# A new written order for a fused RWKV-style scan and wave-mixing kernel on one core

## The chip, the cores and the metric

The kernel runs on one core of a Trainium2 chip. The metric is the device time of one execution in microseconds (us). A core has a matrix engine (PE, with a separate row PEld for its weight loads), two elementwise engines that can read the matrix engine's accumulators in PSUM (DVE and ACT), a third one that can only work on SBUF here (POOL, GpSimd), and a queue that issues transfers (SP). Each engine runs its own instructions strictly in the order in which the program lists them and waits on semaphores for the others.

## The reference

For each of 4 x 8 batch-heads a 40 x 40 state is carried over 768 steps; the outputs, laid side by side as a 4 x 768 x 320 tensor `x`, go through a mixing layer:

```
for t in range(S):
    y[t] = r[t] @ state
    Sa   = state @ a[t]
    state = state * w[t] - outer(Sa, b[t]) + outer(v[t], k[t])
theta = x @ w_theta
y = w_tok_r @ (x * cos(theta)) + w_tok_i @ (x * sin(theta))   # over tokens
u = x + y
out = u + relu(u @ w_ch)
```

## The kernel before, in words

The 768 steps are cut into six chunks of 128 for each of the four batches: 24 chunks, numbered 0 to 23. A chunk holds all eight heads. Inside a chunk the recurrence becomes matmuls on a 128 x 128 scale. The decay is summed on PE from log w and exponentiated on ACT (`CSE`, `CSI`, `WI`, `INVW`, once for two chunks); POOL, and for chunks 0 and 1 DVE, multiplies k and b by one decay (`KH`, tile kb) and a by the other (`AH`, tile ah). PE transposes these (`TRK`, `TRA`, `TRV`, `TRR`), DVE or ACT copies the transposes out of PSUM (`EKBT` to kbT, `EAT` to aT, `EVT` and `ERT` to rvT). Four score matrices per chunk (`PSI`, `PHI`, `LV`, `LU`) are triangular: DVE evicts one with a multiplication by a mask (`EPSI` and so on with V), or ACT evicts it as it is (with A) and POOL then zeroes the other half (`MPSI`, `MPHI`, `MLV`, `MLU`). Solved values (`X0`, `NU`), the carried state (`GT`, `EGT`, `GD`, `EGD`) and the output x (`Y`, `EX`) follow. The old state is added to the new one either by a matmul with the identity (`GI`, function `gt_old`) or by an addition on DVE (`EGA`, function `add_gt`).

The mixing layer follows chunk by chunk: x is transposed (`XT`, `EXT`, or `EXT` with S by a transposing transfer on SP), multiplied by w_theta (`TH`), copied (`ETH`), put through the sine table twice on ACT (`SIN`), and multiplied by x on POOL (`ZR`, tile z). `YR:i.j` adds the share of chunk j to the token mix of chunk i, two matmuls of 320 columns; `EU` adds x, `UT` and `EUT` transpose u, `CH` and `CHR` multiply by w_ch, `EO` makes the output and `ST` stores it. The token-mix sums of chunks 18 to 21 lie in pairs, 18 with 19 and 20 with 21, in one PSUM tile each (the tiles sc0 and sc1, kept in `pairs`); the others have a bank of their own.

What sets the order is one string, `ORDER`. Each entry names a step, its chunk, the engine (A, V, G for POOL, S for a transposing transfer) and a PSUM bank (after @), and the program is recorded in that order with `keep_in_program_order`; nothing is rescheduled. Input loads (`LD..`) stand in the same string, so their order against each other is fixed too. In the names of the trace, sm tiles are single banks and sc tiles two banks; a wait on an sc tile is a wait on the whole tile.

ACT holds one function table at a time: one with ln and exp, one with sin. `ln_exp` loads the first where the last one loaded was another, with a written instruction; before the change the sine table was loaded by one that the compiler puts ahead of a sine.

Of the kernel before, what the change touches and what calls it, by code (L numbers as in the profile page):

```python
# [15 lines left out]
LN_EXP = "natural_log_exp_and_others"  # L16


ORDER = """
LDW:2 LDW:0 LDK:0 LDA:1 LDC:0.0G LDC:0.2G LDA:0 LN:0A LDB:0 CSE:0@0 CSI:0@1 LN:2A CST:0 LDB:1 LDK:1  # L20
INVW:0A WI:0A LDK:2 AH:0V CSI:2@1 CSE:2@0 AH:1V KH:0V CST:2 LDB:2 TRA:0@0 TRK:0@3 LDV:0 EAT:0A
INVW:2A LDR:0 EKBT:0V LDA:2 WI:2A KH:1V PHI:0@1 EPHI:0A PSI:0@0 LDV:1 KH:2G TRA:1@2 EPSI:0V TRK:1@1
EKBT:1V LDB:3 CV:0A MPHI:0G EAT:1A X0:0@0 TRK:2@3 EKBT:2V LDK:3 ENX:0A LDA:3A CR:0A PHI:1@1 PSI:1@0
EPHI:1V LDV:2 AH:2G TRV:0@2 EPSI:1A TRR:0@1 NU:0 LDW:4 EVT:0V ENU:0A TRA:2@3 MPSI:1G GT:0@0 CV:1A
EAT:2V EGT:0V ERT:0A NUT:0@2 LDR:2 PSI:2@0 ENUT:0A PHI:2@1 EPSI:2A TRV:1@3 EPHI:2V KH:3G X0:1@0
LDA:4A ENX:1A LDB:4 LV:0@0 NU:1 EVT:1A LU:0@1 CV:2G ENU:1A ELV:0V TRK:3@2 MPSI:2G ELU:0A NUT:1@3
LDK:4 ERT:1V GT:1@0 GI:1 ENUT:1V LN:4A LV:1@0 LU:1@1 MLU:0G EGT:1V TRV:2@1 LDV:3 X0:2@3 CR:2G ELV:1A
Y:0@0 ELU:1V ENX:2A CSI:4@0 AH:3G LDB:5 EX:0V CSE:4@1 LDA:5A INVW:4A EKBT:3V CST:4 MLV:1G TRA:3@0
LDK:5 WI:4A TRR:2@2 EAT:3V NU:2 EVT:2A ERT:2V KH:4G PSI:3@0 EPSI:3V PHI:3@1 ENU:2A ERT:3A GD:0@0
GT:2@1 LDR:4 NUT:2@3 EGD:0A GI:2 ENUT:2V EPHI:3A LDW:6 TRK:4@2 AH:4G EGT:2V LU:2@0 EKBT:4V CV:3A  # L30
LV:2@1 MPHI:3G X0:3@0 ELU:2A TRA:4@3 Y:1@1 ELV:2V MLU:2G LDA:6A ENX:3A NU:3 EAT:4V TRV:3@2 LDV:4
ENU:3A LDK:6 EX:1V GD:1@3 PHI:4@0 EVT:3V KH:5G PSI:4@1 EGD:1A GT:3@0 EPSI:4A EPHI:4V NUT:3@1 Y:2@2
CR:4G ENUT:3V LN:6A LV:3@0 LDB:6 EX:2V LU:3@1 ELU:3V TRK:5@3 MPSI:4G ELV:3A TRR:4@1 ERT:4A AH:5G
GI:3 GD:2@2 EGT:3V CSE:6@0 LDV:5 CSI:6@1 EGD:2A EKBT:5V CV:4G INVW:6A TRA:5@0 LDK:7 MLV:3G X0:4@2
ENX:4A ERT:5V CST:6 EAT:5V TRV:4@3 XT:1@1 LDB:7 WI:6A XT:0@0 EVT:4V NU:4 KH:6G LDR:6 PHI:5@1 EXT:1A
EXT:0V PSI:5@0 LDA:7A ENU:4A EPHI:5V TH:0@3 AH:6G EPSI:5A NUT:4@0 TRK:6@1 ENUT:4V LDW:8 EKBT:6V
LV:4@1 MPSI:5G LU:4@0 Y:3@2 LDV:6 SIN:0A CV:5G ELU:4V GT:4@0 GI:4 TRV:5@1 KH:7G EGT:4V LDA:8A ELV:4A
EVT:5V MLV:4G TH:1@3 X0:5@0 EX:3V XT:2@1 SIN:1A LDB:8 LV:5@0 TRA:6@2 ENX:5V EXT:2V ELV:5A GD:3@3
EAT:6V TH:2@1 NU:5 CR:6G SIN:2A EGD:3V MLV:5G PSI:6@1 PHI:6@0 ENU:5V EPSI:6V LDV:7 Y:4@2 NUT:5@3
LDK:8 TRR:6@0 ENUT:5V CV:6G EPHI:6V LN:8A TRK:7@1 X0:6@3 LDA:9A ENX:6A AH:7G LU:5@1 ZR:1G LDB:9  # L40
LDK:9 CSE:8@0 ERT:7A ELU:5V NU:6 CST:8 ERT:6A ENU:6A TRA:7@0 ZR:2G EKBT:7V WI:8A AH:8G LDW:10
CSI:8@1 EAT:7V GD:4@3 INVW:8A TRV:6@1 EX:4V PSI:7@0 PHI:7@1 NUT:6@0 EVT:6V EPSI:7V GT:6@2 KH:8G
# [93 lines left out]
def kernel(  # L136
# [14 lines left out]
    nc = tc.nc  # L151
# [176 lines left out]
    table = [LN_EXP]  # L328
# [575 lines left out]
```

## Time and profile before

| | |
|---|---|
| median of three runs | 203.98 us (203.97 to 203.99) |
| profiled execution: its own time, its span | 204.92 us, 203.2 us |
| PE busy | 187.2 us of the span |
| DVE busy | 169.7 us |
| ACT busy | 150.6 us |
| POOL busy | 148.0 us |
| transfers | 35.95 MB, mean 177 GB/s |

The profiled execution is 0.94 us longer than the median, and 1.72 us of it lie outside the span. Busy shares are means over stages with different limits: the head is filled by loads, the first hundred microseconds by elementwise work of the scan, the rest by matmuls of the mixing layer. A PE row's duration includes the way of the last column through the array, so consecutive matmuls overlap in the rows and the distance between two starts says more than a duration.

### The profile page before, as it was taken

The numbers are of one execution on the slowest core, as the hardware profiler recorded it, in microseconds if no ns is written. First come the engines' busy times: TensorE is split into PE (matmuls) and PEld (weight loads), VectorE is DVE, ScalarE is ACT, GpSimd is POOL, SyncE is SP. The second block draws the span as 40 slices with busy tenths as digits, with TensorE's granted clock in tenths as the row PEclk, the third lists the DMA queues.
The fourth block names the chain that finished last, engine by engine and source line by source line (L and its number), as shares of the span: only waits on it lengthen the run. The fifth ranks groups of instructions, "written<-read, shape, count | busy, mean of one in ns | idle before, by whom it ended". The sixth has DMA issues, their size and how long they took to land.

```text
span 203.2 us, 7841 instructions
## 1 busy us (share of the span) xinstructions
PE 187.2 (92%) x3282; PEld 147.9 (73%) x3282; DVE 169.7 (84%) x324; ACT 150.6 (74%) x273; POOL 148.0 (73%) x155
## 2 busy tenths in 40 slices
PE   0669999999999999999999999999999999999892
PEld 0357778877877888787887877877777887777570
DVE  7067889999999998999889899889788888863653
ACT  2556988999899888997999676996798877364110
POOL 8126899999999976998995996974899483762000
PEclk9999999999999999999999999999999999999999
DMA  6999999899899899999878997698793995332523
GB/s 159 169 187 199 207 172 215 137 236 166 163 275 256 158 286 205 243 230 220 224 197 185 236 209 133 135 211 204 145 172 59 218 169 93 77 70 54 194 77 129
DMA packets 141956, 35.95 MB, mean 177 GB/s; under 512 B 136353, under 2 KB 140385, under 8 KB 141921
## 3 DMA queue, kind: packets, MB, share of 16 engines
q1 hardware_dynamic: 120064, 31.57, 73.9%
q10 hardware_dynamic: 20800, 3.28, 9.6%
q0 software_dynamic: 1056, 0.61, 2.2%
q8 instruction: 25, 0.41, 1.0%
q14 instruction: 11, 0.08, 0.2%
HBM read 29.54 MB, written 3.93 MB: 165 GB/s over the span
## 4 chain that ended last, share of the span: by engine, by line
PE 70%; DVE 9%; DMA 7%; ACT 7%; SPq 2%; issue 2%; POOL 1%; ACTq 0%; DVEq 0%; POOLq 0%
PE sm L312 37%; PE sm L316 17%; PE sc L312 16%; DMA raw_v<-in_v_dram 3%; DMA raw_a<-in_a_dram 3%; SPq L363 1%; DVE phi L309 1%; DMA uT<-u_two 1%; DVE lamu L309 1%; DVE rvT L301 1%; ACT lamv L299 1%; ACT cs L737 1%; DVE kbT L301 1%; ACT rvT L299 1%; POOL kb L309 1%
## 5 line engine op out<-in xcount | busy, mean ns | idle before, releaser
L309 POOL TENSOR_TENSOR kb<-raw_kb,invW_two 128x640 bf16<-128x640 f32 x22 | 34.0, 1544 | 13.7 <-DMA raw_kb<-in_b_dram 9.9
L309 POOL TENSOR_TENSOR z<-cs,x_two 128x640 bf16<-128x640 f32 x22 | 30.8, 1404 | 6.9 <-ACT cs L737 5.7
L312 PE MATMUL sm<-z,wtok_r 128*128 128x320 bf16 x120 | 34.6, 300 | 0.0
L312 PE MATMUL sm<-z,wtok_i 128*128 128x320 bf16 x120 | 34.5, 299 | 0.0
L309 DVE TENSOR_TENSOR phi<-sc,mask_p 128x1024 bf16<-128x1024 f32 x17 | 20.7, 1220 | 2.7 <-PE sc L312 2.5
L309 POOL TENSOR_TENSOR ah<-raw_a,Wi_two 128x320 bf16<-128x320 f32 x22 | 19.0, 866 | 3.1 <-issue 2.2
L309 DVE TENSOR_TENSOR psi<-sc,mask_p 128x1024 bf16<-128x1024 f32 x15 | 18.3, 1218 | 0.6 <-PE sc L312 0.5
L312 PE MATMUL sc<-aT,kbT 64*128 64x128 bf16 x384 | 17.0, 225 | 0.9 <-DVE kbT L301 0.8
L309 DVE TENSOR_TENSOR lamu<-sc,mask_p 128x1024 bf16<-128x1024 f32 x14 | 17.1, 1220 | 0.3
L312 PEld LDWEIGHTS <-wtok_r 128*128 128x128 bf16 x144 | 14.0, 97 | 4.6 <-issue 0.5
L312 PEld LDWEIGHTS <-wtok_i 128*128 128x128 bf16 x144 | 14.1, 98 | 4.5 <-issue 1.3
L312 PEld LDWEIGHTS <-rvT 64*128 64x128 bf16 (+1 forms) x272 | 13.8, 94 | 3.5 <-issue 1.4
L312 PEld LDWEIGHTS <-kbT 64*128 64x128 bf16 x384 | 11.7, 98 | 5.8 <-issue 3.4
L316 PE MATMUL sm<-ident,kb 128*128 128x128 bf16 x184 | 15.3, 231 | 0.6 <-DVE kb L309 0.5
L301 DVE COPY kbT<-sm 128x1024 bf16<-128x1024 bf16 x20 | 13.7, 685 | 2.2 <-PE sm L316 2.1
L594 POOL TENSOR_SCALAR_AFFINE_SELECT lamv<-lamv 128x1024 bf16<-128x1024 bf16 x13 | 14.2, 1094 | 1.2 <-ACT lamv L299 1.2
L312 PE MATMUL sm<-kb,lamv 128*128 128x40 bf16 x192 | 15.0, 180 | 0.0
L312 PE MATMUL sm<-kb,lamu 128*128 128x40 bf16 x192 | 14.9, 179 | 0.0
L299 ACT CAST lamv<-sc 128x1024 bf16<-128x1024 f32 x13 | 13.2, 1012 | 1.1 <-PE sc L312 0.8
L312 PE MATMUL sm<-wch,uT 128*128 128x320 bf16 x72 | 13.5, 300 | 0.3 <-DVE uT L301 0.2
L309 DVE TENSOR_TENSOR lamv<-sc,mask_p 128x1024 bf16<-128x1024 f32 x11 | 13.4, 1220 | 0.4 <-PE sc L312 0.4
L312 PE MATMUL sm<-wth,xT 128*128 128x320 bf16 x72 | 13.7, 299 | 0.0
(137 smaller groups left out, 609.7 us busy)
## 6 DMA issues: line engine op xcount, KB each, us to landing
raw_w_two<-in_w_dram SPq DMA_DIRECT2D x12, 320.0 KB, 4.8
raw_kb<-in_k_dram SPq DMA_DIRECT2D x24, 160.0 KB, 4.8
raw_kb<-in_b_dram SPq DMA_DIRECT2D x24, 160.0 KB, 4.6
raw_v<-in_v_dram SPq DMA_DIRECT2D x24, 160.0 KB, 4.9
raw_r_two<-in_r_dram SPq DMA_DIRECT2D x12, 320.0 KB, 5.2
out_dram<-oo SPq DMA_DIRECT2D x24, 160.0 KB, 2.2
raw_a<-in_a_dram ACTq DMA_DIRECT2D x20, 160.0 KB, 5.2
wtok_raw<-in_moe_w_tok_r_dram SPq DMA_DIRECT2D x6, 384.0 KB, 4.6
```

The lines of the kernel that those rows point to most:

```text
L299: keep(nc.scalar.copy(out=out, in_=in_))
L301: keep(eng[e].tensor_copy(out=out, in_=in_))
L309: keep(eng[e].tensor_tensor(out=out, in0=in0, in1=in1, op=ALU.mult))
L312: keep(nc.tensor.matmul(out, lhsT=lhsT, rhs=rhs, start=start, stop=stop, skip_group_check=True))
L316: keep(nc.tensor.transpose(out=out, in_=in_, identity=ident))
L363: transfer(queue(e).dma_start(out=tiles[i].raw_kb[:, j], in_=source(ap, i)))
L594: keep(nc.gpsimd.affine_select(out=flat, in_=flat, compare_op=ALU.is_ge, fill=0.0, base=-1, pattern=[[0, 2 * G], [1, 128]], channel_multip ...
L737: keep(nc.scalar.activation(out=cs[i % 5][:, c], in_=tiles[i].theta, func=AF.Sin, bias=(math.pi / 2, 0.0)[c]))
```

## The change

The string is written anew: 1434 entries where there were 1438. The input loads keep their order against each other; the stores and the transposing transfers stand elsewhere between them. Steps change engine: of the 23 `EKBT` evictions by an engine 13 are now on ACT (3 before), of the 24 `EAT` 14 (6), of the 16 `EGD` 7 (13), of the 24 `ENU` 13 (19); ACT casts no more than 3 `CR` (6) and 2 `CW` (3), the rest being POOL's. The masked evictions on DVE are 61 (57 before), those on ACT with a mask step on POOL 35 (39). Five states are added by a matmul (9 before) and 11 on DVE (7). `KH`, `AH` and `ZR` are on the engines on which they were. Two lines of code differ: `sines` loads the sine table by a written instruction where the other one is loaded, and a pair's tile is taken by the first of its two sums instead of the even one.

```diff
 ORDER = """
-LDW:2 LDW:0 LDK:0 LDA:1 LDC:0.0G LDC:0.2G LDA:0 LN:0A LDB:0 CSE:0@0 CSI:0@1 LN:2A CST:0 LDB:1 LDK:1
+LDW:2 LN:2A LDW:0 CSI:2@1 LDK:0 INVW:2A CSE:2@0 LDA:1 LDC:0.0G LDC:0.2G CST:2 LN:0A WI:2A CSE:0@1
...
     def sines(i):
-        table[0] = None
+        if table[0] != SINE:
+            keep(nc.scalar.preload_act_table_set(SINE))
+            table[0] = SINE
...
             else:
-                if j % 2 == 0:
+                if j // 2 not in pairs:
                     pairs[j // 2] = banks(b).rearrange("p a b c -> p a (b c)")
```

Three places show what moves. The first is the start of ACT's queue: the logarithms (lw_two) of the pairs 0/1 (number 93) and 2/3 (number 94), their exponentials, and the first evictions. Before:

```order
L375 ACTIVATE lw_two_0_93<-raw_w_two_210 128x16x40
L375 ACTIVATE lw_two_1_94<-raw_w_two_208 128x16x40
L410 ACTIVATE invW_two_245<-sc1_227 128x640
L452 ACTIVATE Wi_two_247<-sc0_222 128x656
L299 COPY aT_290<-sm0_274 128x256
```

And now:

```order
L375 ACTIVATE lw_two_1_94<-raw_w_two_208 128x16x40
L410 ACTIVATE invW_two_220<-sc1_213 128x640
L375 ACTIVATE lw_two_0_93<-raw_w_two_211 128x16x40
L452 ACTIVATE Wi_two_241<-sc0_222 128x656
L452 ACTIVATE Wi_two_264<-sc1_243 128x656
L410 ACTIVATE invW_two_274<-sc0_259 128x640
L299 COPY aT_291<-sm0_286 128x256
L299 COPY kbT_318<-sm0_304 128x512
```

The pair 2/3 now goes first, its exponential stands ahead of the logarithm of the pair 0/1, and a kbT is copied on ACT.

The second place is the start of DVE's queue behind the memsets: the products of chunks 0 and 1 and the first transposes. Before:

```order
L309 TENSOR_TENSOR ah_0_95<-raw_a_218,Wi_two_247 128x8x40
L309 TENSOR_TENSOR ah_1_96<-raw_a_214,Wi_two_247 128x8x40
L309 TENSOR_TENSOR kb_0_97<-raw_kb_212,invW_two_245 128x16x40
L301 COPY kbT_296<-sm3_279 128x1024
L309 TENSOR_TENSOR kb_1_98<-raw_kb_242,invW_two_245 128x16x40
```

And now:

```order
L309 TENSOR_TENSOR ah_1_96<-raw_a_227,Wi_two_264 128x8x40
L309 TENSOR_TENSOR ah_0_95<-raw_a_257,Wi_two_264 128x8x40
L301 COPY aT_281<-sm0_276 128x512
L309 TENSOR_TENSOR kb_0_97<-raw_kb_218,invW_two_274 128x16x40
L309 TENSOR_TENSOR kb_1_98<-raw_kb_268,invW_two_274 128x16x40
L301 COPY kbT_320<-sm3_294 128x1024
```

Chunk 1's ah goes first and its kb now stands ahead of the copy of chunk 0's kbT.

The third place is near the end of PE's queue: the last token-mix matmuls of chunks 18 and 19, which share one sc0 tile, the first transposes of chunk 18's u (u_two_0), and the products with w_ch between them. Before:

```order
L312 MATMUL sm3_5101<-wch_201,uT_5059 128x320
...
L312 MATMUL sc0_5027<-z_1_199,wtok_i_206 128x320
...
L312 MATMUL sc1_5018<-z_1_199,wtok_r_205 128x320
...
L316 MATMUL sm1_5126<-ident_58,u_two_0_117 128x128
```

And now:

```order
L312 MATMUL sc0_4954<-z_1_199,wtok_i_206 128x320
...
L312 MATMUL sm3_5106<-wch_201,uT_5101 128x320
L312 LDWEIGHTS uT_5101
L312 MATMUL sm1_5122<-wch_201,uT_5101 128x320
...
L312 MATMUL sc1_5005<-z_1_199,wtok_r_205 128x320
...
L312 MATMUL sm2_5001<-z_1_199,wtok_r_205 128x320
...
L316 MATMUL sm1_5137<-ident_58,u_two_0_117 128x128
...
L312 MATMUL sc0_4954<-z_1_199,wtok_r_205 128x320
```

In the old order `YR:18.5`, `EU:18`, `YR:19.5` follow each other with one `YR` of two matmuls (`YR:19.4`, on the same tile) between the first two; in the new one four products with w_ch, six token-mix matmuls of other tiles and two transposes stand between `EU:18` and `YR:19.5`.

More of the change, by code (lines that the diff above doesn't have):

```diff
@@ L16 @@
 LN_EXP = "natural_log_exp_and_others"
+SINE = "trig_and_small"
 ORDER = """
-LDW:2 LDW:0 LDK:0 LDA:1 LDC:0.0G LDC:0.2G LDA:0 LN:0A LDB:0 CSE:0@0 CSI:0@1 LN:2A CST:0 LDB:1 LDK:1
[L21 to L30, printed above, removed]
@@ new lines @@
+EU:0V ENX:10A TRK:11@1 LN:12A NU:10 ELV:10V TH:6@3 CSE:12@1 CW:2.1G MLU:9G EX:8V ENU:10A EKBT:11V
+CSI:12@0 CST:12 LDW:14 LDK:13 ETH:6A GT:10@2 WT:2.1@3 INVW:12A LDB:13 WI:12A WT:2.0@1 EWT:2.1V
+EGA:10V LDA:13A Y:9@0 EWT:2.0A NUT:10@3 XT:8@1 PHI:11@1 KH:12G EGT:10V EXT:8A LDT:3.0 ENUT:10A
+PSI:11@0 YR:2.0@1 EX:9V CV:11A EPSI:11V YR:2.1 XT:9@2 YR:2.2 TRV:11@0 EPHI:11A TRK:12@3 EXT:9V
+EVT:11V X0:11@2 LN:14A LU:10@1 AH:12G LDC:0.4G LV:11@0 LDV:12 MPHI:11G EKBT:12V ELU:10V TRA:12@0
+LDC:0.6G LDR:12 AH:13G ELV:11V YR:2.3 YR:2.4 ENX:11A KH:13G LDA:14A YR:1.0@3 EAT:12A CW:3.0G TH:8@0
@@ new lines @@
+ETH:8V NU:11 YR:2.5 YR:1.1 EU:2V SIN:6A PSI:12@0 PHI:12@1 ENU:11A EPSI:12V YR:1.2 SIN:7A LDB:14
+GD:9@1 LDT:3.1 EPHI:12V TRA:13@2 NUT:11@0 LDK:14 YR:1.3 EAT:13V YR:1.4 CV:12G EGD:9A SIN:8A YR:1.5
+ENUT:11A TRK:13@1 CR:12G LDC:0.5G EKBT:13A CSI:14@0 LU:11@1 LDV:13 X0:12@0 LDC:0.7G EU:1V INVW:14A
+WT:3.0@1 ELU:11V ENX:12V Y:10@3 LDV:14 TRR:12@2 LDR:14 PSI:13@1 LDK:15 NU:12 EWT:3.0V CW:3.1G
+ERT:12A CSE:14@0 EX:10V LDA:15A CST:14 EPSI:13V ENU:12A TRV:12@3 GD:10@1 KH:14G GT:12@0 ERT:13A
+EVT:12V CV:13G LDB:15 WT:3.1@2 WI:14A EGD:10A EWT:3.1A PHI:13@1 LV:12@0 EGT:12V NUT:12@3 ELV:12V
@@ new lines @@
+X0:20@1 ERT:21A YR:9.4 ERT:20V YR:9.5 LN:22A ENX:20V TH:15@3 EU:9V GD:19@2 ST:7 NU:20 EGD:19V
+LV:20@0 ENU:20V CSE:22@1 UT:9@0 YR:11.0@2 SIN:15A CST:22 GT:20@3 YR:11.1 ELV:20V LDB:22 YR:11.2
+WI:22A YR:11.3 EGA:20V CV:21A YR:11.4 MLU:19G AH:22G YR:11.5 PSI:21@0 CSI:22@1 ST:0 CH:8@1 EGT:20V
+EU:11V EUT:9A ENUT:20S EPSI:21V CHR:9@2 CH:9 INVW:22A TRA:22@0 TRV:21@3 EXT:17S PHI:21@1 MLV:19G
+LU:20@0 EO:8V ST:4 EVT:21V EAT:22A ELU:20V TH:17@0 EPHI:21A KH:22G YR:13.0@3 ETH:17A YR:13.1
+TRK:22@1 SIN:16A ZR:15G YR:13.2 EUT:10S MPHI:21G EKBT:22V Y:19@0 LV:21@1 EO:9V UT:11@1 EX:19V
```

193 lines of the change are left out of this document (92 added, 101 removed).

## The prediction

> **What bounds the kernel now.** I read the page first, then the busy time by stage, then what PE waits for, then rows in time at both ends.
>
> ```profile
> span 203.2 us, 7841 instructions
> PE 187.2 (92%) x3282; PEld 147.9 (73%) x3282; DVE 169.7 (84%) x324; ACT 150.6 (74%) x273; POOL 148.0 (73%) x155
> PE   0669999999999999999999999999999999999892
> DVE  7067889999999998999889899889788888863653
> ```
>
> PE is full from the fourth slice to the last three, DVE nearly full up to the middle. A table of stages separates them; the columns are PE, PEld, DVE, ACT and POOL busy time with instruction counts, the clock, and the transfers.
>
> ```profile
> 0.00:20.00 20.00, 11.12 (x130) 8.11 (x131) 11.55 (x54) 9.76 (x16) 9.05 (x20) 1.00 1.01 179
> 20.00:60.00 40.00, 38.40 (x823) 31.18 (x822) 38.09 (x65) 37.27 (x66) 37.84 (x39) 1.00 1.02 196
> 60.00:100.00 40.00, 39.45 (x784) 32.45 (x781) 37.92 (x58) 35.15 (x69) 35.34 (x37) 1.00 1.10 234
> 100.00:180.00 80.00, 79.89 (x1402) 63.53 (x1400) 71.38 (x130) 63.49 (x113) 62.51 (x60) 1.00 0.79 158
> 180.00:203.20 23.20, 18.37 (x154) 12.68 (x152) 10.78 (x23) 4.89 (x14) 3.24 (x3) 1.00 0.35 108
> ```
>
> From 20 to 100 us DVE is busy 38.09 + 37.92 = 76.0 of 80 us and ACT 37.27 + 35.15 = 72.4: the scan's evictions pace PE. From 100 to 180 us PE is idle for 0.11 us in all and DVE for 8.6: PE sets the pace. PE loses 8.9 us in the first 20 us and 4.8 in the last 23. The waits of PE name two causes of size:
>
> ```profile
> PE sc L312 <- ACT lw_two L375: 6.1, 1, 6.1
> PE sc L312 <- DVE u_two L765: 0.9, 2, 0.6
> ```
>
> The first is the head, until the first load has come and its logarithm is made; the second lies in the last stretch. So four terms: the head, the paced first hundred, the matmul stage, the end.
>
> **The head.** Loads keep their order, and ACT's queue now has the exponential of pair 2/3 (`INVW:2`) ahead of the logarithm of pair 0/1 (`LN:0`). Behind `LN:0` wait `CSE:0` on PE, `WI:0` on ACT and the first products on DVE. Rows: a load's time to landing, then instructions with start and duration; the third is a row of the chain of waits.
>
> ```profile
> raw_w_two<-in_w_dram SPq DMA_DIRECT2D x1, 320.0 KB, 3.2
> 5.35 1.36 ACT L375 ACTIVATE lw_two<-raw_w_two 128x640 bf16<-128x640 f32 x2 [3.27 <-DMA raw_w_two<-in_w_dram]
> 3.91 6.05 DMA raw_a<-in_a_dram
> 10.06 0.89 DVE L309 TENSOR_TENSOR ah<-raw_a,Wi_two 128x320 bf16<-128x320 f32 x2 [4.60 <-DMA raw_a<-in_a_dram]
> 12.82 0.69 DVE L301 COPY kbT<-sm 128x1024 bf16<-128x1024 bf16 x1 [1.13 <-PE sm L316]
> ```
>
> The first load (pair 2/3) is issued at 0.8 us and has landed at 4.0; before, its logarithm stood behind the one of pair 0/1, whose load came at 5.3. Now it runs from 4.0 to 4.7, its sums on PE take 0.8 us, `INVW:2` is done near 6.4, `LN:0` runs to 7.1, then sums and `WI:0`, together as long as from 6.7 to 8.7 before, to some 9.2 us. The load of chunk 0's a lands at 3.91 + 6.05 = 9.96 in both orders, so the 1.0 us that `LN:0` comes later is hidden behind that load, with 0.7 us to spare. Chunk 1's ah goes ahead of it for nothing. On DVE the copy of aT and the kb of chunk 1 now stand ahead of the copy of chunk 0's kbT: 0.4 + 0.8 us, in the 1.13 us in which DVE waited for PE before. I take 0. The ends: -1.0, if chunk 1, whose kb and kbT come earlier now, fills PE's gaps between 13 and 20 us; +0.8, if both insertions on DVE (1.2 us) delay the first scores and only 0.4 of it finds cover.
>
> **The first hundred.** I counted the entries ahead of the last output of batch 2 (`EX:11`) in both strings and priced the difference with the grouped rows (busy, mean ns, idle before):
>
> ```profile
> L301 DVE COPY kbT<-sm 128x1024 bf16<-128x1024 bf16 x20 | 13.7, 685 | 2.2 <-PE sm L316 2.1
> L299 ACT COPY kbT<-sm 128x512 f32<-128x512 f32 x3 | 1.8, 588 | 0.7 <-PE sm L316 0.7
> L301 DVE COPY aT<-sm 128x512 bf16<-128x512 bf16 x18 | 7.5, 419 | 1.1 <-PE sm L316 0.9
> L299 ACT COPY aT<-sm 128x256 f32<-128x256 f32 x6 | 2.2, 373 | 3.6 <-PE sm L316 3.6
> L301 DVE CAST gd<-sm 128x320 bf16<-128x320 f32 x3 | 1.5, 484 | 0.3 <-PE sm L312 0.3
> L299 ACT CAST gd<-sm 128x320 bf16<-128x320 f32 x13 | 5.6, 431 | 2.5 <-PE sm L312 2.5
> L563 DVE TENSOR_SCALAR nu<-sm 128x320 bf16<-128x320 f32 x5 | 2.4, 490 | 1.0 <-PE sm L312 0.9
> L644 DVE TENSOR_TENSOR sm<-sm,gt 128x320 f32<-128x320 f32 x7 | 3.4, 491 | 0.3 <-PE sm L312 0.3
> L309 DVE TENSOR_TENSOR phi<-sc,mask_p 128x1024 bf16<-128x1024 f32 x17 | 20.7, 1220 | 2.7 <-PE sc L312 2.5
> L299 ACT CAST lamv<-sc 128x1024 bf16<-128x1024 f32 x13 | 13.2, 1012 | 1.1 <-PE sc L312 0.8
> L299 ACT CAST wtok_row<-wtok_raw 128x768 bf16<-128x768 f32 x3 | 2.5, 833 | 0.0
> L301 DVE COPY rvT<-sm 128x512 bf16<-128x512 bf16 x23 | 12.3, 546 | 0.5 <-ACT rvT L299 0.4
> L312 PE MATMUL sm<-gt,ident 128*128 128x320 bf16 x9 | 2.7, 300 | 0.0
> ```
>
> DVE: kbT -7 x 0.685 = -4.8, aT -4 x 0.419 = -1.7, gd +4 x 0.484 = +1.9, state additions +3 x 0.491 = +1.5, masked evictions +1 x 1.22, nu +2 x 0.490 = +1.0; six small copies change by one, net four fewer at 0.35 to 0.55, -1.8. Together -2.7 us. ACT: kbT +7 x 0.588 = +4.1, aT +4 x 0.373 = +1.5, gd -4 x 0.431 = -1.7, row casts -2 x 0.833 = -1.7, evictions -1.0, small ones +1.4: +2.6 us. POOL has less to do up to there too.
>
> With the busy times above, DVE falls from 76.0 to 73.3 and ACT rises from 72.4 to 75.0. The later one of the two went from 76.0 to 75.0. That is -1.0, and I take -0.9, since two engines near their limit meet more often than one. The ends: -2.7 if ACT's idle time (7.6 us in these 80) swallows its new work; +2.6 if that idle time is all waits for PE in ACT's fixed order and stays, so that its new work is paid in full. PE's own work ahead of that point is the same but for three `GI`.
>
> Rows against rule: a copy of kbT takes 0.685 us on DVE and 0.588 on ACT here. The Trainium skill, "ScalarE: Activation LUTs", section "Rules for kernel authors", gives cheap elementwise work to VectorE, which it calls up to about three times faster per element in bf16. By that rule the seven copies would cost ACT up to 7 x 3 x 0.685 = 14.4 us instead of 4.1, an estimate, and the change would be a loss of some 9 us; the rows contradict it for these copies.
>
> **The matmul stage.** Four `GI` go, one of them (chunk 13) where PE sets the pace. Its row says 0.300 us, but starts of 320 columns lie 0.135 apart (rows below): -0.1. The order within is new; with PE idle for 0.11 us in 80 I take neither gain nor loss; the bounds are 0 (a gain is the second rival) and +1.1, twice the 0.55 us that PE loses in the 40 us from 60 to 100.
>
> **The table.** Loads before:
>
> ```profile
> L737 ACT ACT_TABLE_LOAD x7 | 9.0, 1283 | 0.1
> L332 ACT ACT_TABLE_LOAD x6 | 7.7, 1283 | 0.1
> ```
>
> The new program has seven and six again, each directly ahead of a sine or an exponential on the same queue: 0.
>
> **The end.** Rows of PE, and one of the chain of waits (second):
>
> ```profile
> 188.12 0.97 PE L312 MATMUL sm<-wch,uT 128*128 128x320 bf16 x4
> 186.18 2.42 DMA uT<-u_two
> 188.93 0.30 PE L312 MATMUL sc<-z,wtok_r 128*128 128x320 bf16 x1
> 189.88 0.30 PE L312 MATMUL sc<-z,wtok_i 128*128 128x320 bf16 x1
> 190.76 0.30 PE L312 MATMUL sc<-z,wtok_r 128*128 128x320 bf16 x1 [0.58 <-DVE u_two L765]
> 190.90 0.30 PE L312 MATMUL sc<-z,wtok_i 128*128 128x320 bf16 x1
> 192.40 0.43 PE L312 MATMUL sm<-wch,uT 128*128 128x320 bf16 x2
> 193.14 0.30 PE L312 MATMUL sc<-z,wtok_r 128*128 128x320 bf16 x1 [0.31 <-DVE u_two L765]
> ```
>
> From 190.76 to 190.90 is one matmul: 0.135. The row at 190.76 is `YR:19.5`, which writes the tile that `EU:18` reads; it starts 0.88 after the one at 189.88, so 0.75 is lost. `YR:21.1` at 193.14 waits for `EU:20` alike: 0.74 from 192.40 less two matmuls, 0.47 lost. The four products at 188.12 need 0.54 and the next starts after 0.81: 0.27 lost, on chunk 17's u, whose transfer lands at 186.18 + 2.42 = 188.60. Sum 1.49.
>
> In the new order twelve matmuls of 0.135 stand between the end of `YR:18.5` and `YR:19.5`, ten of them 320 columns wide: 1.4 us, against 0.3 of matmul tail and 0.49 of `EU` (with another `EU` of 0.49 ahead of it). Between `YR:20.5` and `YR:21.2` there are six: 0.8 us, against the same 0.8. `EU:17` is made much earlier, but its transfer now stands behind that of chunk 23's x on SP, so the 0.27 may stay. What would be late next is the chain behind the last output: `Y:23`, `EX:23`, a transposing transfer of 2.3 to 2.5 us, `TH:23`, sines, `ZR:23`. Between `Y:23` and `TH:23` stand twelve pairs of matmuls and `TH:22`, 12 x 0.27 + 0.41 = 3.65 us, for 0.3 + 0.49 + 2.42 + handovers, 3.4 us; it just fits. I take -1.3 of the 1.49; the ends are -1.5 and +0.9, if that chain comes 2.4 us late, the length of one more transfer ahead of it, while only the 1.49 is saved.
>
> **Sum.** 0 - 0.9 - 0.1 + 0 - 1.3 = -2.3 us. The profiled execution has a span of 203.2 and 1.72 us around it, 204.92 in all; it would take 202.6. It lay 0.94 above the median of the runs, so I forecast 203.98 - 2.3 = **201.7 us**.
>
> **The rivals.**
> - *The end alone* (0.14). The first hundred returns nothing, because ACT and DVE now block each other as often as DVE alone did: -1.3 - 0.1, 202.6 us. For it: ACT's row total of 75.0 is within 1.0 of the old limit. Against: POOL has slack.
> - *PE has hidden slack* (0.10). A row of 0.300 us at a distance of 0.135 hides waits shorter than the difference, so PE may be paced by DVE to the end. Then DVE's -2.7 counts in full, with -1.5 at the end: 203.98 - 4.2 = 199.8 us. For it: PEld is at 73% where PE is at 92%. Against: PE's idle time of 0.11 us in 80. The Trainium skill, "Perfetto Trace Analysis", section "Identifying the Most-Contended Engine", says that matmul busy time is a poor measure of headroom and that weight-load busy time is to be used; by that rule DVE at 84% is the bound throughout, and this rival follows.
> - *ACT becomes the bound* (0.22), the other side. Place: 20 to 100 us, ACT's queue. Its order is fixed, and a kbT copy waiting for PE holds up the evictions behind it. If its 7.6 us of idle time remain, the stage ends 2.6 us later; less 1.4 at the end and by `GI`, that is +1.2: 205.2 us. It decides once more than about 1.4 us of the added work is paid. Against: POOL and DVE release ACT's inputs sooner.
> - *No net change* (0.12). About half of ACT's added work is paid, +1.3, against -1.4: 203.9 us. That the sine table's new line does nothing is part of every case.
>
> **How the numbers follow.** The forecast has 0.42, its own range being 200.8 to 202.6. Differences under 0.2%, 0.4 us, cannot be told from none here. Faster: 0.42 + 0.14 + 0.10 = 0.66; same 0.12; slower 0.22. For 8 in 10 the range runs from 199.8, the hidden slack, to 205.2, the ACT case, which leaves out about half of each of these two, 0.05 and 0.11.
>
> **What would show it.** Right: in the changed profile no wait of PE for u_two of more than 0.2 us behind 185 us; from 20 to 100 us DVE and ACT both near 75 us busy and PE's busy time there above 78; the first kbT copy still near 12.8 us; thirteen table loads of 1283 ns behind the first one. Wrong: PE idle between 20 and 100 us grown by more than 1 us with ACT as releaser (the ACT case), or a wait of PE for z or xT behind 190 us (the last chain). The forecast falls with any stage from 100 to 180 us in which PE is idle for more than 1 us.

## The result

The changed kernel takes 202.18 us (median of 4 runs, 201.96 to 202.44) against 203.99 (203.97 to 204.14): a ratio of 0.991, with a 95% interval of 0.9893 to 0.9927, 1.8 us. The forecast was 201.7, within its own range of 200.8 to 202.6. The profiled execution took 202.4 us where the one before took 204.92, and its span is 2.5 us shorter; the sum of the prediction was -2.3. Some 0.7 us of the 2.5 is scatter: the profiled execution before lay 0.94 above its median, the one after 0.22. The sum was right. Its terms were not, as the next sections show.

From the page of the changed kernel, the span, the busy times and the slices of PE and DVE; then the busy time by stage (columns as before: PE, PEld, DVE, ACT, POOL):

```profile
span 200.7 us, 7824 instructions
PE 186.6 (93%) x3278; PEld 147.8 (74%) x3278; DVE 168.7 (84%) x319; ACT 149.2 (74%) x278; POOL 146.5 (73%) x155
PE   0769999999999999999999999999999999999992
DVE  7257899899999998999899899899999876862682
```

```profile
0.00:20.00 20.00, 11.94 (x134) 8.57 (x135) 11.60 (x54) 9.87 (x15) 10.14 (x21) 1.00 1.09 182
20.00:60.00 40.00, 38.65 (x834) 31.84 (x832) 37.66 (x62) 38.19 (x70) 34.95 (x35) 1.00 1.07 199
60.00:100.00 40.00, 39.93 (x786) 32.63 (x782) 38.22 (x59) 36.10 (x74) 36.83 (x39) 1.00 1.11 231
100.00:180.00 80.00, 80.00 (x1398) 63.68 (x1398) 70.75 (x124) 60.13 (x109) 60.69 (x60) 1.00 0.81 155
180.00:200.70 20.70, 16.11 (x139) 11.06 (x136) 10.51 (x23) 4.87 (x13) 3.89 (x3) 1.00 0.41 129
```

From 20 to 100 us PE is busy for 78.6 us (77.85 before), DVE for 75.9 and ACT for 74.3. The prediction's sums had 73.3 for DVE and 75.0 for ACT, so DVE's did not come. PE has four instructions fewer, the four `GI`. The 8 in PE's slices near the end, where it waited for u_two, has become a 9.

**Where the time went.** Busy shares in fixed windows do not say which part of the program a window holds. So I laid the two traces side by side by PE's own work: each matmul counts as the time for which it occupies PE (0.136 us for 320 columns, 0.056 for 128, as the distances of starts show), these are added in the order of the starts, and the time is read at which a given sum is reached. What a stretch takes above its work is waiting and the switches of row count described at the end. Work that goes anywhere in the program shows in the third row, since the others hold a fixed amount of it. The last column is the prediction's term.

| stretch, by PE's work | before | after | difference | predicted |
|---|---|---|---|---|
| to 25 us of work (the first 41 us) | 40.70 | 40.88 | +0.18 | 0 |
| 25 to 80 us of work (41 to 100 us) | 60.14 | 58.82 | -1.32 | -0.9 |
| from there to the last 20 us of work (100 to 177 us) | 76.44 | 75.30 | -1.14 | -0.1 |
| the last 20 us of work | 22.02 | 21.80 | -0.22 | -1.3 |
| start of the last matmul | 199.30 | 196.80 | -2.50 | -2.3 |

Of the -1.14, 0.55 is work that is gone (four matmuls of 0.136; three of them stood in the first hundred). The first and the last row are single executions of stretches that scatter, by up to 1.4 and 0.4 us between executions of the new order.

The switches of row count are not the same in the two orders: 15, 26, 24 and 1 groups of matmuls with 64 rows lie in the four stretches before, 18, 30, 24 and 2 after. At 0.19 us for each group the new order pays some 0.6, 0.8, 0 and 0.2 us for them, an estimate, so the waiting fell by more than the table shows. Added up from the distances of starts, PE loses 3.4 us between 41 and 100 us before, beyond work and switches, and 1.3 us after. The longest single loss before, 0.60 us, is this one, a matmul that waits for an rvT whose copy stands behind a masked eviction on DVE:

```profile
58.06 1.22 DVE L309 TENSOR_TENSOR lamu<-sc,mask_p 128x1024 bf16<-128x1024 f32 x1
59.19 0.41 DVE L301 COPY rvT<-sm 128x512 bf16<-128x512 bf16 x1
59.66 0.40 PE L312 MATMUL sc<-rvT 64*128 64x128 bf16 x8 [0.43 <-DVE rvT L301]
```

Two more of 0.5 us, at 49 and 92 us, are ended by DVE too; after the change no loss there is longer than 0.37 us.

The end gave a sixth of what was promised. This is why: rows of PE near 185 us, first the changed kernel's list of PE's waits behind 176 us, then the rows in time.

```profile
PE sm L312 <- DMA xT<-x_two: 0.8, 2, 0.4
PE sm L312 <- ACT uT L299: 0.2, 1, 0.2
```

```profile
184.24 0.30 PE L312 MATMUL sc<-z,wtok_i 128*128 128x320 bf16 x1
184.96 0.58 PE L312 MATMUL sm<-wth,xT 128*128 128x320 bf16 x3 [0.43 <-DMA xT<-x_two]
...
186.06 0.30 PE L312 MATMUL sm<-z,wtok_i 128*128 128x320 bf16 x1
186.73 0.58 PE L312 MATMUL sm<-wth,xT 128*128 128x320 bf16 x3 [0.37 <-DMA xT<-x_two]
```

No wait for u_two is left. But `TH:22` starts 0.72 us behind the matmul ahead of it and `TH:23` 0.67, where 0.136 would do: 0.59 + 0.53 = 1.1 us is lost to the transposed x of the last two chunks. SP's queue at that time (start, duration of the issue) shows one reason, with the row of DVE that makes x of chunk 23:

```profile
180.34 1.20 SPq L701 DMA_TRANSPOSE xT<-x_two  x1
181.59 2.67 SPq L780 DMA_DIRECT2D out_dram<-oo  x2
184.36 1.18 SPq L701 DMA_TRANSPOSE xT<-x_two  x1
...
182.12 0.49 DVE L309 TENSOR_TENSOR x_two<-sm,Wi_two 128x320 bf16<-128x320 f32 x1 [0.25 <-PE sm L312]
```

x of chunk 23 is ready at 182.6, but two stores (`ST:12`, `ST:8`) hold the queue from 181.59, so its transfer is issued at 184.36.

### The profile page after: what moved, and what is told of

It reads as the page before. It is cut to its first block, busy times and chain, and to the rows that moved or that the text cites. A ratio compares the mean times of both kernels' runs of the same rounds, so it can differ in the third digit from the quotient of the medians.

```text
span 200.7 us, 7824 instructions
## 1 busy us (share of the span) xinstructions
PE 186.6 (93%) x3278; PEld 147.8 (74%) x3278; DVE 168.7 (84%) x319; ACT 149.2 (74%) x278; POOL 146.5 (73%) x155
## 4 chain that ended last, share of the span: by engine, by line
PE 83%; SPq 5%; DVE 5%; DMA 4%; issue 1%; ACT 0%; DVEq 0%; ACTq 0%
PE sm L312 42%; PE sm L316 21%; PE sc L312 20%; DMA raw_kb<-in_k_dram 3%; SPq L363 1%; SPq L780 1%; DVE psi L309 1%; DMA xT<-x_two 1%; DVE phi L309 1%; SPq L368 1%; SPq L701 1%; DVE lamv L309 1%; DVE lamu L309 1%; SPq L357 1%; DVE kb L309 0%
## 5 line engine op out<-in xcount | busy, mean ns | idle before, releaser
L309 DVE TENSOR_TENSOR psi<-sc,mask_p 128x1024 bf16<-128x1024 f32 x18 | 21.9, 1217 | 1.5 <-PE sc L312 1.5
L309 DVE TENSOR_TENSOR phi<-sc,mask_p 128x1024 bf16<-128x1024 f32 x16 | 19.5, 1219 | 1.6 <-PE sc L312 1.3
L309 DVE TENSOR_TENSOR lamu<-sc,mask_p 128x1024 bf16<-128x1024 f32 x15 | 18.3, 1219 | 0.5 <-PE sc L312 0.3
L312 PE MATMUL sc<-aT,kbT 64*128 64x128 bf16 x384 | 17.5, 225 | 0.0
L299 ACT COPY rvT<-sm 128x512 bf16<-128x512 bf16 (+1 forms) x26 | 12.7, 500 | 5.0 <-PE sm L316 4.9
L309 DVE TENSOR_TENSOR lamv<-sc,mask_p 128x1024 bf16<-128x1024 f32 x12 | 14.6, 1219 | 0.3
L776 DVE SCALAR_TENSOR_TENSOR oo<-sm,u_two 128x320 f32<-128x320 f32 x24 | 10.9, 489 | 3.6 <-PE sm L312 3.5
L309 DVE TENSOR_TENSOR x_two<-sm,Wi_two 128x320 bf16<-128x320 f32 x24 | 11.7, 486 | 2.5 <-PE sm L312 2.4
L594 POOL TENSOR_SCALAR_AFFINE_SELECT lamv<-lamv 128x1024 bf16<-128x1024 bf16 x12 | 13.1, 1092 | 0.9 <-ACT lamv L299 0.7
```

Of the source, the lines that this page charges most:

```text
L299: keep(nc.scalar.copy(out=out, in_=in_))
L309: keep(eng[e].tensor_tensor(out=out, in0=in0, in1=in1, op=ALU.mult))
L312: keep(nc.tensor.matmul(out, lhsT=lhsT, rhs=rhs, start=start, stop=stop, skip_group_check=True))
L594: keep(nc.gpsimd.affine_select(out=flat, in_=flat, compare_op=ALU.is_ge, fill=0.0, base=-1, pattern=[[0, 2 * G], [1, 128]], channel_multip ...
L776: keep(nc.vector.scalar_tensor_tensor(out=q.oo, in0=q.ops[:, 0:DM], scalar=0.0, in1=q.u, op0=ALU.max, op1=ALU.add))
```

## The experiments

They ran on other chips than the first comparison; there the kernel before took 205.0 to 205.7 us with a spread of some 3 us, so a ratio is known to 0.2 to 0.5% either way, and effects under 1 us are read from the traces, by PE's work as above. In that reading the middle of the kernel is mostly the same from one execution to the next: from 25 us of work to the last 20 it took 134.11 to 134.13 us in four traces that have the new order there (the changed kernel twice, x4_fill and x5_stores). A fifth, x6_pe, differs: its matmuls start 0.98 us later than those of after_again at 110 us and 1.56 us later at 171, though the orders are equal up to there. The lost 0.6 us stand as two waits, one behind a product of POOL that waited 0.45 us for its load, one for a product ah of POOL. All runs, those with the old order too, have the two changed lines of code.

### Four orders put together from the two

Each ends with a piece of one order as it stands; ahead of it come all other steps, in the sequence that the other order gives them. So a step that the end already has is missing from its old place.

**s1_new_then_old** and **s2_old_then_new** are joined near 100 us:

```diff
 # s1_new_then_old: the new order, up to
 ... YR:3.5 EU:3V EVT:14A ZR:8G PHI:14@1 KH:15G EPHI:14V CW:4.1A
-LDA:16A EGD:12A EGA:13V ELU:13A TRK:15@1 CW:4.0G ...
+ERT:14A CH:0@1 ENUT:13V CHR:1@2 CH:1 EPSI:14A LDV:15 ...
```

> The new order for the steps of roughly the first 100 us, the old order behind them. Theory by stages (read from the two traces at equal work of PE): the first hundred returns 1.1 us and the three GI that go in it 0.4, so 1.5 us under the kernel before, some 202.5 us. By the prediction's terms: 0.9 for the first hundred and nothing for these GI, 203.1. Rival, that the orders only pay together (the lead of the first hundred is lost again by the time the old end begins): within 0.3 us of before.

> The old order for the first 100 us, the new one for the matmul stage and the end. Theory by stages: 0.5 us from the matmul stage, 0.4 from the end, 0.1 from one GI, so 1.0 us under before, some 203.0 us. By the prediction's terms (0.1 and 1.3): 1.4 us under before, 202.6. Rival, that all of the gain was made in the first hundred: 204.0.

**s3_new_old_end** and **s4_old_new_end** are joined near 178 us:

```diff
 # s4_old_new_end: the old order, up to
 ... YR:17.0@3 YR:17.1 YR:17.2 YR:17.3 YR:17.4 YR:17.5 EU:17V
-YR:18.1 YR:19.0 YR:19.1 EO:14V EO:15V EUT:17S ...
+TH:20@3 ENUT:23A EUT:14S YR:18.0@0 EUT:15S ZR:19G LU:23@1 ...
```

> The new order up to about 178 us, the old end behind it. Theory by stages: the new end is worth only 0.4 us, because the waits for chunk 18's and 20's EU were traded for waits on the transposed x of chunks 22 and 23; so some 0.4 us above the changed kernel, 202.6 us, with the old waits back in the trace (two for u_two, 0.9 us in all). By the prediction's term the end is worth 1.3: 203.5.

> The old order up to about 178 us, the new end alone. Theory by stages: 0.4 us under before, 203.6 us, with waits of PE for the transposed x of the last two chunks. By the prediction's term for the end: 1.3 us under before, 202.7. Rival, that the last chain comes late altogether: slower than before by up to 0.9, 204.9.

Measured, as ratios to the kernel before: s1 1.0016 (0.9987 to 1.0045), s2 1.0066 (1.0043 to 1.0089), s3 1.0019 (0.9997 to 1.0042), s4 1.0002 (0.9973 to 1.0031). No mixture is faster than the kernel before, though each holds a part of the gain. The theories of s1, s2 and s3 were missed; s1 came out about as its rival said, that the orders only pay together. The 0.4 us expected of s4 lie within its interval, but in its trace the last 20 us of work take 22.3 us, not less than the 22.02 before. The traces show PE waiting at the joint; one row of PE from each of the four, in the order s1, s2, s3, s4:

```profile
101.78 0.58 PE L304 MATMUL sm<-wch,uT 128*128 128x320 bf16 x3 [0.90 <-DVE nuT L293]
```

```profile
105.03 0.62 PE L308 MATMUL sm<-ident,kb 128*128 128x128 bf16 x8 [1.33 <-POOL kb L301]
```

```profile
178.51 0.40 PE L304 MATMUL sc<-rvT,nuT 64*128 64x128 bf16 x8 [0.57 <-ACT nuT L291]
```

```profile
181.93 0.57 PE L304 MATMUL sm<-wth,xT 128*128 128x320 bf16 x3 [0.58 <-DVE u_two L759]
```

By PE's work, s1 takes 53.52 us from 25 to 75 us of work like the changed kernel (53.54; before 54.90), then 6.99 for the next 5 us of work instead of 5.24 or 5.28, and its last 20 us take 22.02, as before. So its first part did return 1.4 us, and the joint took 1.7. A joint removes matmuls that stood between a step and the one that needs its result; in s2 PE waits 1.33 us for a kb that POOL has only just made. The expectations treated stages as parts whose gains add; these runs do not bear that out, since each stage lends work to the next. How much of each run's loss is the joint was worked out for s1 alone.

### The end of the old order alone

**x3_pairs** leaves the old order up to the end and moves there only what stood behind the shared sums:

```diff
-YR:18.5 EO:17V YR:19.4 ST:16 EU:18V YR:19.5 YR:20.3 ST:17 EU:19V YR:20.4 UT:18@1 YR:20.5 UT:19@0 EUT:18A YR:21.1 EU:20V ...
+YR:19.4 YR:18.5 EU:18V EO:17V ST:16 YR:20.3 YR:20.4 YR:21.1 YR:21.2 YR:21.3 YR:19.5 ST:17 EU:19V UT:18@1 YR:20.5 EU:20V ...
```

> The old order with only the end's matmuls moved so that YR:19.5 and YR:21.1 no longer stand right behind the sums that EU:18 and EU:20 read; TH:22 and TH:23 stay where they were. Theory (the two waits of PE for u_two cost 0.75 and 0.47 us of PE and nothing else was late there): 1.2 us under before, 202.8 us. Rival, that the shared tile's waits were slack, with the end set by the transfers of u and the stores: within 0.3 us of before.

Ratio 0.9946 (0.9914 to 0.9978), -1.1 us, and the last 20 us of PE's work take 20.69 us instead of 22.02: -1.33. The list of PE's waits behind 176 us has one entry left:

```profile
PE sm L304 <- DVE uT L293: 0.2, 1, 0.2
```

The prediction's price for the old waits, 1.49 of which 1.3 would be had, is right where nothing else is moved.

### What holds the new end

**x4_fill** moves sums into the waits of `TH:22` and `TH:23`:

```diff
-YR:19.2 ZR:21G EO:14V TH:22@3 ... YR:23.2 TH:23@3 YR:18.2 YR:19.3 EO:15V YR:18.3 ... YR:20.5 EU:20V ST:15 YR:18.5 ... EU:18V
+YR:19.2 ZR:21G EO:14V YR:18.2 YR:21.2 TH:22@3 ... YR:23.2 YR:18.3 YR:21.3 TH:23@3 YR:19.3 EO:15V ... YR:18.5 EU:18V ST:15 YR:20.5 ... EU:20V
```

> The new order with six token-mix sums moved within the last 20 us: YR:18.2 and YR:21.2 ahead of TH:22, YR:18.3 and YR:21.3 ahead of TH:23, YR:22.3 earlier, and YR:18.5 with EU:18 ahead of YR:20.5 with EU:20. Theory (the end gave back 1.1 us to the waits of TH:22 and TH:23 for transposed x): 4 pairs of matmuls, 4 x 0.27 = 1.1 us of work, now stand in these waits, so up to 1.1 us under the changed kernel, 201.1 us. Rival, that another link of the last chain (z of chunk 23, or the last stores) sets the end: within 0.3 us of the changed kernel.

**x5_stores** moves `ST:12 ST:8` behind `EXT:23S`, nothing else:

```diff
-ZR:20G ST:12 SIN:21A ... CHR:15@1 ST:8 YR:20.1 ... EXT:23S EUT:16S
+ZR:20G SIN:21A ... CHR:15@1 YR:20.1 ... EXT:23S ST:12 ST:8 EUT:16S
```

> The new order with the two stores ST:12 and ST:8 moved behind the transposing transfer of chunk 23's x on SP's queue; nothing else. Theory (these two stores hold SP for 2.67 us from 181.59 on, while x of chunk 23 is ready at 182.6): the transfer is issued 1.7 us earlier, the wait of TH:23 (0.54 us lost) goes, and that of TH:22 (0.59) shrinks if the stores also slow the transfer of chunk 22's x, which takes 4.6 us to land: between 0.5 and 1.1 us under the changed kernel. Rival, that the transfer waits for something else, or that the end is set by a later link: within 0.3 us of the changed kernel.

**x6_pe** transposes x of the chunks 22 and 23 on PE:

```diff
-EXT:22S ... TH:21@3 YR:21.1 ETH:21V ... ST:8 YR:20.1 YR:20.2 ... EXT:23S
+TH:21@3 XT:22@1 YR:21.1 EXT:22V ETH:21V ... ST:8 YR:20.1 XT:23@0 YR:20.2 EXT:23V
```

> The new order with x of chunks 22 and 23 transposed by PE and copied by DVE in place of the transposing transfers; YR:20.0 and YR:23.0 change places for the bank that this needs. Theory (PE's two waits at the end are the transfers' latency): 1.13 us of waits go, six transposes of 0.06 us come, so some 0.8 us under the changed kernel and no wait for transposed x in the trace. Rival, that the time goes to the next link (z of chunk 22 or 23, the transposes of u), as when sums were moved into the gaps: within 0.3 us of it.

**after_again** is the changed kernel on the chip of x5 and x6.

> The changed kernel once more, as the measure for the three runs beside it on the same chip. Every theory: 0.991 of the kernel before. If the ratio is under 0.988, the changed kernel gains more on a chip where the kernel before takes longer, and the runs before this one have to be read against that.

| kernel | ratio to before | last 20 us of PE's work |
|---|---|---|
| after_again | 0.9894 (0.9847 to 0.9940) | 21.36 |
| x4_fill | 0.9876 (0.9832 to 0.9920) | 21.59 |
| x5_stores | 0.9874 (0.9836 to 0.9913) | 21.26 |
| x6_pe | 0.9903 (0.9864 to 0.9942) | 21.45 |

The changed kernel repeats its ratio. By time none of the three can be told from it. The traces tell what each did. In x4_fill no wait for xT is left, and four new ones have come; PE's rows, where each second start lies 0.33 to 0.41 behind the first instead of 0.136:

```profile
188.63 0.30 PE L304 MATMUL sm<-z,wtok_i 128*128 128x320 bf16 x1
189.03 0.43 PE L304 MATMUL sm<-wch,uT 128*128 128x320 bf16 x2
...
192.19 0.30 PE L304 MATMUL sc<-z,wtok_i 128*128 128x320 bf16 x1
192.60 0.45 PE L304 MATMUL sm<-wch,uT 128*128 128x320 bf16 x2
```

The sums that fill the first gaps are missing as cover for the transposes of u: 0.26 + 0.20 + 0.28 + 0.19 = 0.93 of the 1.1 us comes back. That is its rival's claim, though the link is another than the two that it named. In x5_stores the transfer of chunk 23's x is issued at 182.88, as soon as x is ready (it shares a row of SP's queue with chunk 22's), and of the two waits for xT one is left, that of `TH:22`:

```profile
180.65 3.75 SPq L693 DMA_TRANSPOSE xT<-x_two  x2
184.45 1.04 SPq L772 DMA_DIRECT2D out_dram<-oo  x2
...
PE sm L304 <- DMA xT<-x_two: 0.3, 1, 0.3
```

That is as the theory said: x of chunk 23 lands 2.70 us after it is ready, 4.08 and 3.64 in the two traces of the changed kernel, and the end is 0.54 shorter than in the first of them. (Against after_again it is 0.1, because there the wait of `TH:22` happened to be short.) One trace does not prove it: in x2_gi_back below `TH:23` did not wait either, with the stores where the changed kernel has them. And chunk 22's x still takes 4.4 us to land with no store behind it, so the stores are not what slows it. In the changed kernel it took 4.6 us in one execution and 3.7 in the other, and in x4_fill, with the same order on SP, 2.4; what decides between 2.4 and 4.6 stays open. (So x4_fill does not show that its sums alone would have covered `TH:22`.) In x6_pe the transfers are gone, and `TH:22` waits for a product on DVE, whose row stands behind a copy of xT:

```profile
186.28 0.57 PE L304 MATMUL sm<-wth,xT 128*128 128x320 bf16 x3 [0.30 <-DVE oo L768]
...
185.47 0.36 DVE L293 COPY xT<-sm 128x384 bf16<-128x384 bf16 x1 [1.31 <-PE sm L308]
185.75 0.48 DVE L768 SCALAR_TENSOR_TENSOR oo<-sm,u_two 128x320 f32<-128x320 f32 x1
```

`EO:14` frees the bank that `TH:22` writes. In this order it stands on DVE behind `EXT:23`, which waits 1.31 us for PE. In x4_fill and x6_pe the next link takes most of what the repair of one link gave.

### The four GI

**x2_gi_back** adds four states by matmuls again:

```diff
-EGA:3V ... EGA:9V ... EGA:10V ... EGA:13V
+GI:3 ... GI:9 ... GI:10 ... GI:13
```

> The new order with the states of chunks 3, 9, 10 and 13 added by matmuls with the identity again and not on DVE. Theory (each GI costs PE 0.135 us and PE is full from 20 us on): 4 x 0.135 = 0.5 us above the changed kernel, 202.7 us. Rival, that DVE's 4 x 0.49 = 2.0 us less count as well, since PE follows DVE in the first hundred: between 1.5 us under the changed kernel and 0.2 under it.

Ratio 0.9864 (0.9827 to 0.9901), by time not to be told from the changed kernel. From 25 us of work to the last 20 it takes 134.66 us, 0.54 above the 134.12 of the changed kernel: exactly 4 x 0.136. So all four were paid by PE, and DVE's 2.0 us less (four additions of 0.49) bought nothing. The end then took 21.26, 0.1 to 0.5 less than the changed kernel's, since `TH:23` did not wait in this trace. Here the two stores held SP for 1.04 us and the transfer's own issue for 2.20; in the changed kernel's traces it was 2.67 and 1.79 for the stores and 1.18 for the transfer. What makes the difference is not shown. In sum the last matmul starts at 196.97, within 0.2 of the changed kernel's first trace.

### The kbT copies

**x1_kbt_back** puts ten kbT copies of the new order back on DVE, **x8_old_kbt** moves the same ten of the old order to ACT:

```diff
 # x1_kbt_back: the new order; x8_old_kbt: the old order with the reverse
-EKBT:1A EKBT:2A EKBT:4A EKBT:5A EKBT:7A EKBT:8A EKBT:13A EKBT:15A EKBT:16A EKBT:23A
+EKBT:1V EKBT:2V EKBT:4V EKBT:5V EKBT:7V EKBT:8V EKBT:13V EKBT:15V EKBT:16V EKBT:23V
```

> The new order with the ten kbT copies that went to ACT back on DVE. Theory (the first hundred pays because DVE has less work): DVE gets 7 x 0.685 = 4.8 us more up to 100 us, ACT 4.1 less; DVE's total of 75.9 of 80 us leaves 4.1 of idle time, so between 0.7 and 3 us above the changed kernel, 203 to 205 us. Rival, that the order of the steps and not the engines makes the gain: less than 0.4 us above it.

> The old order, unchanged but for the ten kbT copies that the change moves from DVE to ACT. Theory (the later one of the two queues paces the first hundred): DVE 76.0 - 4.8 = 71.2, ACT 72.4 + 4.1 = 76.5 of 80 us, so 0.5 us above the kernel before. First rival, that DVE alone paces (putting these ten back cost the new order over 4 us): 1.5 to 4 us under before. Second rival, that ACT's queue becomes the bound where its steps stand in an order made for less work: 1 to 3 us above before.

x1: 1.0134 (1.0093 to 1.0174), over 4 us above the changed kernel and above all that was expected. x8: 1.0200 (1.0161 to 1.0238), 4.1 us above the kernel before. The same ten copies cost over 4 us in either direction, taken alone. The theory of queue totals (0.5 us for x8) falls, and so does the first rival, that DVE alone paces: DVE had its work taken away in x8 and the kernel became slower. The second rival (1 to 3 us) named the right side but not the right size or cause: ACT is not full. Its stages, columns as above:

```profile
20.00:60.00 40.00, 37.68 (x804) 31.30 (x803) 34.51 (x57) 37.19 (x67) 35.90 (x35) 1.00 1.05 199
60.00:100.00 40.00, 38.90 (x767) 31.69 (x766) 38.07 (x59) 35.50 (x69) 35.24 (x39) 1.00 0.99 207
```

DVE 72.6 and ACT 72.7 of 80 us: both have room, and yet PE is busy for 76.6 us only, against 77.85 before. What costs is who stands behind a copy that waits. First in x8, ACT and PE; then the same two steps in the kernel before:

```profile
16.29 0.58 ACT L291 COPY kbT<-sm 128x512 f32<-128x512 f32 x1 [0.81 <-PE sm L308]
16.77 0.46 ACT L291 CAST v<-raw_v 128x320 bf16<-128x320 f32 x1
...
17.29 0.42 PE L304 MATMUL sm<-v,psi 128*128 128x40 bf16 x8 [1.03 <-ACT v L291]
```

```profile
15.12 0.46 ACT L299 CAST v<-raw_v 128x320 bf16<-128x320 f32 x1
...
15.99 0.45 PE L312 MATMUL sm<-v,psi 128*128 128x40 bf16 x8
```

The copy of chunk 1 waits for its transposes, the cast of v for chunk 0 stands behind it on ACT, and the solve that needs v starts 1.3 us later, 1.03 of it as a wait for v. In x1 it is DVE, with the changed kernel's rows behind:

```profile
14.24 1.29 DVE L293 COPY kbT<-sm 128x1024 bf16<-128x1024 bf16 x2 [1.13 <-PE sm L308]
...
15.59 1.03 PE L304 MATMUL sc<-aT,kbT 64*128 64x128 bf16 x16 [1.38 <-DVE kbT L293]
```

```profile
13.08 0.68 DVE L301 COPY kbT<-sm 128x1024 bf16<-128x1024 bf16 x1
...
14.18 1.04 PE L312 MATMUL sc<-aT,kbT 64*128 64x128 bf16 x16
```

In the new string `EKBT:1` stands ahead of `EKBT:0`. On two engines they run beside each other; on one, chunk 0 waits for chunk 1's transposes and then for its copy, and the first scores start 1.4 us later.

The pattern comes again further down. In x1 at 58 us PE waits 1.11 us for a nuT whose copy stands on DVE behind a kbT copy that waited 0.71 us for PE; in x8 at 109 us it waits 1.07 us for a th that stands on ACT behind a kbT copy that waited 0.86 us. These four waits of PE are about half of what the two runs lose; the rest is in smaller pieces.

## Why the prediction was right in sum, and where it was wrong

- **The head, 0.** Not contradicted: +0.18 in the first trace, -0.32 in the second, with a scatter of 1.4 us between executions. DVE's first kbT copy came at 13.08, 12.82 before, and `INVW:2` was done at 6.34 where 6.4 was foreseen. The prediction did not name two waits of DVE ahead of that copy, 0.47 and 0.56 us, for the loads of a b and a k.
- **The first hundred, -0.9.** Measured -1.32 from 41 to 100 us. From 25 to 75 us of work seven traces of the new order take 53.5 us, four of the old one 54.7 to 55.3. The sign and about the size are right, but the step that gave them failed: "The later one of the two went from 76.0 to 75.0." After the change DVE still shows 75.9 of 80 us, and x8_old_kbt showed that with both totals under 73 of 80 the stage takes longer. What sets the pace is which waiting instruction stands ahead of which on a queue: PE's losses in this stretch fell from 3.4 to 1.3 us. The ten kbT copies pay because the string was written for them, and neither half does without the other; the other changes of engine were not tested alone. A second step failed: "PE's own work ahead of that point is the same but for three `GI`." Seven more groups with 64 rows stand there (46 for 39), some 1.3 us by the 0.19 us for each, an estimate. The sum had nothing for them, and the shorter waits paid for them.
- **The matmul stage, -0.1.** Too small by 1.0. 0.41 of that is `GI`: the prediction counted one of four, since it took PE's work in the first hundred as covered; x2_gi_back showed that each costs its 0.136 us. The other 0.59 us was hidden slack: PE's busy time left 0.11 us idle in 80, yet the stage took 76.44 us for 74.55 of work in three traces of the old order, and takes 75.30 for 74.00 in four of the new one. The second rival had this mechanism, with the reason that a row of 0.300 at a distance of 0.135 hides short waits, but not its size. The largest single piece found is 0.27 us at 121 us of the old trace, the others are under 0.12; which steps free them was not tested. Added up from the distances of starts, these losses are 0.64 us before and 0.09 in two traces of the new order, but 0.65 in x6_pe: a late product of POOL can take the gain back.
- **The table, 0.** Thirteen loads of 1283 ns again, behind the first:

```profile
L736 ACT ACT_TABLE_LOAD x7 | 9.0, 1283 | 0.1
L332 ACT ACT_TABLE_LOAD x6 | 7.7, 1283 | 0.1
```

- **The end, -1.3.** The mis-sized term: -0.22, and -0.66 in the second trace. The price of the old waits was right (x3_pairs: 1.33). What failed is the cover: "it just fits". That step gave the last chain one transfer of 2.42 us. It left out two stores ahead of that transfer on SP: x landed 4.08 us after it was ready, 2.70 with the stores behind it (x5_stores). And it did not look at chunk 22, whose transfer took 4.6 us; why that long stays open. The waits stood at 185 and 187 us, earlier than the 190 named as the place to look.

The rivals: the end alone is refuted, since the first hundred and the matmul stage gave most; ACT as the bound did not come to pass in the changed kernel; no net change is refuted by the ratio, at most 0.9927. The forecast held because +1.1 at the end and -1.0 in the matmul stage are about equal. That is luck: no step of the prediction ties the one to the other.

## What to carry to other kernels

In a fully written order an engine assignment and the order are one choice: price a moved copy by the instructions that stand behind it while it waits, not by its 0.6 us in the total of a queue. Before a stall is booked as gained, follow the next two links of the chain on every queue, stores and transfers included; filler taken for one gap is missing from the next. Where PE is full, every matmul counts, wherever it stands, and a busy share of 99.9% still hid 0.6 us that another order saved in most executions.

## What the runs showed of the hardware

**Where the scatter is.** Executions of the new order differ most in the first 41 us and, by the landing of one transfer, in the last 20; between them four of five agree. One early matmul, the `NU` of one chunk, in after_again and in x4_fill, whose orders are equal up to there:

```profile
38.86 0.36 PE L312 MATMUL sm<-nx,phi 128*128 128x40 bf16 x8 [0.30 <-ACT nx L561]
```

```profile
40.23 0.36 PE L304 MATMUL sm<-nx,phi 128*128 128x40 bf16 x8 [0.32 <-ACT nx L553]
```

That is 1.4 us, more than most effects studied here, while the 134.1 us that follow agree to 0.02. The two ran on different chips; after_again and x5_stores, on one chip, are 0.75 us apart at this place. The exception is x6_pe, 0.6 us longer in between, and in the old order the stretch from 25 to 75 us of work scatters by 0.6 us in four traces.

**A switch of the matmul's row count.** Rows of PE in the changed kernel around two groups of eight matmuls with 64 rows:

```profile
99.83 0.30 PE L312 MATMUL sm<-wch,uT 128*128 128x320 bf16 x1
100.07 0.40 PE L312 MATMUL sc<-aT,kbT 64*128 64x128 bf16 x8
100.30 0.39 PE L312 MATMUL sc<-rvT,nuT 64*128 64x128 bf16 x8
100.62 0.32 PE L312 MATMUL sm<-ident,gt 128*128 128x80 bf16 x4
```

Going in, the distance is 0.24 where 320 columns take 0.136. The first group takes 0.23, the second, with the way out, 0.32; between them nothing is lost. That is about 0.1 us each way, 0.19 for a group, and none of it shows as idle. Nearly all switches of the trace have these distances (0.231 to 0.232 us from 320 columns into 64 rows, 0.148 out of 128 columns with 64 rows, where the next pair would start after 0.053). The Trainium skill, "TensorEngine Tiling (Array Packing)", section "Key Properties", says that changing the tiling mode drains the engine; these rows agree and give it a size. In the strings the steps with 64 rows (scores and decay sums) form 66 groups before and 74 after. By the 0.19 us the eight more would cost 1.5 us, an estimate; no run here joined groups to see whether it comes back.
